# The last quarter of each row block ordered by products in the second layer of a dense network

## The chip, the cores and the metric

The kernel runs on one core of a Trainium2 chip. The metric is the device time of one execution in microseconds (us). Matmuls run on TensorE (PE, with its weight loads PEld), elementwise work on VectorE (DVE), ScalarE (ACT) and GpSimd (POOL), and most transfers are issued by SyncE (SP).

## What is computed

Three networks in a row: attention with a window of 128, a mixture of eight experts with two chosen for each token, and a dense network with a squared ReLU. Only the last is touched, and of it the last product:

```python
def _moe2_ref(x, w_in, w_out):       # x: 2304 x 512
    h = x @ w_in                     # w_in: 512 x 2048
    r = np.maximum(h, 0.0)
    g = r * r
    return (g @ w_out).astype(np.float32)   # w_out: 2048 x 512
```

## The kernel before

Each of the two layers of the dense network is computed with a scheme of seven products in place of eight block products: sums and differences of quarters of the operands go in, and sums and differences of the seven results give the quarters of the output. The products are called P1 to P7; their order in the code is P1, P2, P6, P7, P5, P4, P3. Each product of two float32 operands is three matmuls ("passes": high part by high part, high by low, low by high), with operands split into a high and a low part beforehand (helper `mul_out`, L1201; one matmul gives 128x256).

The second layer goes through nine **row blocks** of 256 rows. A row block is named by s (0 to 2) and u (0 to 2). Its seven results are summed in four PSUM banks, each bank holding 512 columns:

- `b13`: P1 in its first half (columns 0:256), P3 in its second
- `b26`: P2 and P6
- `b7`: P7 alone
- `b45`: P4 in the first half, P5 in the second

Row blocks where 3s+u is even ("even": five of nine, the last one among them) have three banks of tag "a" (psa in the profile) and one of tag "c" (psc, which is b45). The odd ones have four halves of tag "b" (psb).

The inner dimension of a row block is taken in four **quarters** (`kk` = 0 to 3, called batches), and each quarter in two **halves** (`k` = 0, 1). A half of a quarter is one turn through the seven products, 21 matmuls; a quarter is 42 matmuls, and a row block 168. The left operands of a quarter lie in one of three buffers `GC` (in the tiles wc and ex); the weights `WP` lie in tiles wa, ha, wb, hb and xa. Which of these a matmul reads shows in its name: psc<-ha,ex is a matmul into b45 of an even row block with weights in ha.

After each product of each half a function `step()` runs side work that is keyed to a slot number, 14 slots to a quarter. The side work of the second layer prepares later quarters (line L872 in the profile): `g_load` (DMA into xb), `g_adds` (sums gs, on POOL or DVE), and `g_split` (ACT writes the high part, DVE the low part, into the buffer GC of the quarter after next). `g_split` has its four parts at slots 2, 5, 8 and 11 of a quarter; parts 0 and 2 are on ACT, parts 1 and 3 on DVE.

The **evictions** of a row block stand in the last half of the last quarter. `p1` is a copy of P1 by ACT (L1242). Then DVE makes x = p1 + (P2, P6) (L1244, 128x512), u3 = x + P7 (L1246), y = u3 + (P4, P5) (L1248, 128x512; then SP writes y out, L1249), x += P5 (L1250) and x += P3 (L1252; then SP writes x out, L1253). In an even row block each of these stands behind the product that it needs last, so that it runs beside the later products; in an odd one all stand behind the last product.

Every engine executes its instructions in the order of the code. Waits between engines are put in by the framework where tiles are shared. The tiles x, y and gs are drawn from one ring of six buffers.

```python
batches = [(0, u, 2 * p + kk) for p in range(2) for u in range(2) for kk in range(2)]
batches += [(s, u, kk) for s in range(NSB) for u in range(3) for kk in range(4) if s or u > 1]
...
def mul_out(p, home, k, kk, o, start, stop):
    for m, (gp, wp) in enumerate(PASSES):
        nc.tensor.matmul(o, (part(home, p[0], gp)[:, kk * 128:(kk + 1) * 128]), (part(WP[k], p[1], wp)),
                         start=start and m == 0, stop=stop and m == 2, skip_group_check=True)
...
for n in range(len(batches)):
    for m in range(2):
        if n + 3 < len(batches):
            on(end + 14 * n + (9 + 3 * m if n < 5 else 1 + 4 * m), g_adds, n + 3, "dve" if n < 5 else "pool", m)
    for m in range(4):
        on(end + 14 * n + (2, 5, 8, 11)[m], g_split, n + 2, m)
```

Of the kernel before, what the change touches and what calls it, by code (L numbers as in the profile page):

```python
# [11 lines left out]
F32 = mybir.dt.float32  # L12
# [4 lines left out]
AF = mybir.ActivationFunctionType  # L17
OP = mybir.AluOpType
# [3 lines left out]
N, DM = B * S, H * D  # L22
# [9 lines left out]
SB = 768  # L32
HALF = 384
# [16 lines left out]
def attn_moe_ffn(ctx: ExitStack, tc: tile.TileContext, qt, kt, vt, wgn, noise, w1, w2, w_in, w_out,  # L50
                 consts, out):
    nc = tc.nc
    PSUM, DRAM = bass.MemoryType.PSUM, bass.MemoryType.DRAM
    const = ctx.enter_context(tc.tile_pool(name="const", bufs=1))
    rows = ctx.enter_context(tc.tile_pool(name="rows", bufs=1))
# [15 lines left out]
    def bank(tag):  # L71
        if tag == "b":
            return psum.tile([128, 2, 512], F32, name="psb", tag="b", bufs=2)
        return psum.tile([128, 512], F32, name="ps" + tag, tag=tag, bufs={"a": 3, "c": 1}[tag])
# [145 lines left out]
    P2, PT, PX, XI, G = {}, {}, {}, {}, {}  # L220
# [294 lines left out]
    for p in range(NT // 2):  # L515
# [6 lines left out]
        o = v + 2 if end else v + 3  # L522
# [30 lines left out]
    for v in range(-2, NV + 3):  # L553
# [4 lines left out]
        if 0 <= v < NV:  # L558
            i, g = divmod(v, 2)
# [242 lines left out]
    P1, P2, P6, P5, P7, P4, P3 = (0, 0), (1, 1), (3, 5), (5, 3), (6, 6), (2, 4), (4, 2)  # L802
# [5 lines left out]
    def spot(t, c0, n):  # L808

        return t[:, c0:c0 + 512 * n].rearrange("p (s i n) -> p s i n", s=2, i=n)  # L810

    WP, XC, tmp = [None] * 8, [None] * 7, []
# [26 lines left out]
    def part(home, i, s):  # L839
        for i0, ap in reversed(home):  # L840
            if i >= i0:
                return ap[:, s, i - i0, :]
# [228 lines left out]
    GC = [[(0, spot(*a, 7))] for a in ((late["wc"], 0), (late["wc"], 3584), (late["ex"], 0))]  # L1071
# [45 lines left out]
    for s in range(NSB - 1):  # L1117
        for i in range(6):
            t, m = 6 * (s + 1) + i, 56 * s + 5 * i + 3
# [22 lines left out]
    def step():  # L1142
        for f, a in side.pop(slot[0], []):
            f(*a)
        slot[0] += 1
# [53 lines left out]
# [4 lines that stand above are left out]
# [11 lines left out]
    two = lambda ap: ap.rearrange("p (k n) -> p k n", k=2)  # L1214
    twice = lambda ap: ap[:, None, :].to_broadcast([128, 2, 256])
    for n, (s, u, kk) in enumerate(batches):
        if kk == 0:
            if (3 * s + u) % 2:
                t = [bank("b") for _ in range(2)]
                banks = [x[:, m, :] for x in t for m in range(2)]  # L1220
            else:
                banks = [bank("a") for _ in range(3)] + [bank("c")]
            BANKS[s, u] = banks
        b13, b26, b7, b45 = BANKS[s, u]
        for k in range(2):
            st, en = kk + k == 0, kk == 3 and k == 1
            for m, (p, o, lead) in enumerate(((P1, b13[:, 0:256], True), (P2, b26[:, 0:256], True),
                                              (P6, b26[:, 256:512], False), (P7, b7[:, 0:256], True),
                                              (P5, b45[:, 256:512], True), (P4, b45[:, 0:256], False),
                                              (P3, b13[:, 256:512], False))):  # L1230
                mul_out(p, GC[n % 3], 2 * kk + k, k, o, st and lead, en)
                if not en:
                    step()
                    continue

                late_ = (3 * s + u) % 2
                if m == 0:
                    p1, u3 = tmp[2 + late_][:, 0:256], tmp[late_][:, 0:256]
                    x, y = [rows.tile([128, DM], F32, name="x", tag="r", bufs=6) for _ in range(2)]
                    i = s * SB + u * 128  # L1240
                if m == (6 if late_ else 0):
                    nc.scalar.activation(out=p1, in_=b13[:, 0:256], func=AF.Copy)  # L1242
                if m == (6 if late_ else 2):
                    nc.vector.tensor_tensor(out=two(x), in0=twice(p1), in1=two(b26), op=OP.add)  # L1244
                if m == (6 if late_ else 3):
                    nc.vector.tensor_tensor(out=u3, in0=x[:, 256:512], in1=b7[:, 0:256], op=OP.add)  # L1246
                if m == (6 if late_ else 5):
                    nc.vector.tensor_tensor(out=two(y), in0=twice(u3), in1=two(b45), op=OP.add)  # L1248
                    nc.sync.dma_start(out=out[i + HALF:i + HALF + 128, :], in_=y)  # L1249
                    nc.vector.tensor_tensor(out=x[:, 256:512], in0=x[:, 256:512], in1=b45[:, 256:512], op=OP.add)  # L1250
                if m == 6:
                    nc.vector.tensor_tensor(out=x[:, 256:512], in0=x[:, 256:512], in1=b13[:, 256:512], op=OP.add)  # L1252
                    nc.sync.dma_start(out=out[i:i + 128, :], in_=x)  # L1253
                step()


def _consts():
# [53 lines left out]
```

## Time and profile before

| | us |
|---|---|
| three runs | 972.5, 975.42, 977.13 (median 975.42) |
| the profiled execution | 974.33 |
| its span, first to last instruction | 972.6 |
| second layer of the dense network, first matmul | 785.82 |
| last quarter of the five even row blocks begins | 811.19, 841.43, 881.75, 922.07, 962.39 |

Start times are counted from the start of the span. A matmul row gives the start of the first matmul and the time to the end of the last; matmuls overlap, so the distance of starts, not the duration, is what one costs. "idle before <-releaser" in a timeline row is how long the engine had nothing to do ahead of it, and what ended this.

### The profile page before, as it was taken

How to read it: one execution, taken by the hardware profiler on the slowest of the kernel's cores; microseconds unless marked ns; L12 is line 12 of the kernel's file. 1: busy time of each engine (PE TensorE's matmuls, PEld its weight loads, DVE VectorE, ACT ScalarE, POOL GpSimd, SP SyncE). 2: the span in 40 equal slices, each digit the busy share in tenths (PEclk: the TensorE clock that was granted, in tenths of full speed). 3: DMA queues.
4: the chain of work that ended last, by engine and by line, in shares of the span. 5: the costliest groups of instructions: out<-in, count | busy, mean ns of one | idle time of the engine just before them, and what ended most of it. 6: DMA issues, size and time to landing. Idle time of an engine off the chain costs nothing. (4 is left out here: it accounts for less than half of the span.)

```text
span 972.6 us, 19636 instructions
## 1 busy us (share of the span) xinstructions
PE 956.8 (98%) x7438; PEld 878.9 (90%) x7438; DVE 668.2 (69%) x1452; ACT 463.2 (48%) x887; POOL 401.8 (41%) x433
## 2 busy tenths in 40 slices
PE   9999999999999999999999999999999999999997
PEld 6777789898998989899898898999999999999997
DVE  5777754657686776757774436778577899877773
ACT  7778733334343443433343346655555564434341
POOL 1565542124232333415334032624211624888880
PEclk9999999999999999999999999999999999999999
DMA  9767525456667576656655453966537874443331
GB/s 324 283 213 271 176 89 155 143 172 215 204 212 233 165 238 193 236 186 210 203 196 192 149 174 94 300 197 175 163 102 222 234 230 156 152 137 125 130 109 44
DMA packets 118199, 180.00 MB, mean 185 GB/s; under 512 B 11232, under 2 KB 66288, under 8 KB 117712
## 3 DMA queue, kind: packets, MB, share of 16 engines
q1 hardware_dynamic: 107120, 146.77, 46.8%
q0 software_dynamic: 10976, 31.90, 10.5%
q8 instruction: 59, 0.97, 0.4%
q14 instruction: 44, 0.36, 0.1%
HBM read 124.33 MB, written 54.30 MB: 184 GB/s over the span
## 5 line engine op out<-in xcount | busy, mean ns | idle before, releaser
L476 ACT ACTIVATE ha<-psa 128x384 fp32r<-128x384 f32 x64 | 31.3, 491 | 94.8 <-PE psa L472 93.2
L872 POOL TENSOR_TENSOR gs<-xb 128x256 f32<-128x256 f32 x62 | 60.2, 992 | 29.3 <-DVE wc L872 15.4
L268 ACT ACTIVATE p<-p,mx 128x192 f32<-128x192 f32 x144 | 57.5, 450 | 27.4 <-DVE mx L262 26.6
L689 POOL TENSOR_TENSOR et<-ex,et 128x512 f32<-128x512 f32 x16 | 20.9, 1304 | 111.5 <-DVE ex L685 111.5
L710 POOL DMA_INDIRECT yr<-yg,pos x36 | 37.3, 1037 | 68.6 <-DVE ha L477 45.1
L477 DVE SCALAR_TENSOR_TENSOR ha<-psa,ha 128x384 fp32r<-128x384 f32 x64 | 35.4, 553 | 42.6 <-ACT ha L476 37.5
L472 PE MATMUL psa<-xa,wa 128*128 128x384 f32 x288 | 55.0, 343 | 0.0
L428 POOL DMA_INDIRECT slots<-tok,pos x36 | 35.0, 972 | 45.7 <-DVE rs L314 30.0
L886 POOL DMA_DIRECT2D raw<-w x49 | 27.2, 561 | 63.5 <-DVE wb L872 18.4
L441 POOL DMA_INDIRECT xr<-xd,gidx x40 | 44.8, 1119 | 20.9 <-issue 6.1
L472 PE MATMUL psa<-xa,wc 128*128 128x384 f32 x288 | 53.3, 335 | 0.0
L791 PE MATMUL psb<-wa,ha 128*128 128x512 f32 x216 | 52.8, 396 | 0.0
L472 PEld LDWEIGHTS psa<-xa,wa 128*128 128x128 f32 x288 | 51.0, 194 | 0.2
L262 DVE CUSTOM_DVE_ANT_0 p<-psb,bias 128x192 f32<-128x192 f32 x144 | 45.8, 352 | 6.1 <-PE psb L257 5.4
L472 PEld LDWEIGHTS psa<-xa,wc 128*128 128x128 f32 x288 | 49.6, 188 | 0.2
L795 ACT ACTIVATE yo<-psb 128x512 f32<-128x512 f32 x38 | 22.7, 598 | 54.4 <-PE psb L791 38.7
L791 PEld LDWEIGHTS psb<-wa,ha 128*128 128x128 f32 x216 | 39.5, 188 | 7.8
L689 POOL TENSOR_TENSOR ex<-ex 128x512 f32<-128x512 f32 x12 | 15.6, 1302 | 74.6 <-DVE ex L685 74.6
L791 PE MATMUL psb<-wb,ha 128*128 128x512 f32 x176 | 46.3, 397 | 0.0
L110 DVE TENSOR_TENSOR wa<-raw,wa 128x1024 fp32r<-128x1024 f32 x20 | 25.7, 1284 | 29.4 <-ACT wa L106 29.3
L872 DVE TENSOR_TENSOR wc<-gs,wc 128x512 fp32r<-128x512 f32 x48 | 44.4, 965 | 0.4 <-ACT wc L872 0.4
L303 PEld LDWEIGHTS psb<-v,pt 64*64 64x64 f32 (+1 forms) x1056 | 32.8, 135 | 11.0 <-issue 7.7
(330 smaller groups left out, 2726.9 us busy)
## 6 DMA issues: line engine op xcount, KB each, us to landing
raw<-in_w_dram SPq DMA_DIRECT2D x64, 512.0 KB, 4.9
xb<-gmid SPq DMA_DIRECT2D x72, 256.0 KB, 2.9
v<-in_vt_dram SPq DMA_DIRECT2D x20, 520.0 KB, 5.3
yg<-yo SPq DMA_DIRECT2D x40, 256.0 KB, 3.1
raw<-w POOLq DMA_DIRECT2D x36, 256.0 KB, 3.8
gmid<-yo SPq DMA_DIRECT2D x48, 192.0 KB, 3.2
ex<-in_w_in_dram SPq DMA_DIRECT2D x16, 512.0 KB, 4.1
ex<-in_w_out_dram SPq DMA_DIRECT2D x16, 512.0 KB, 3.5
```

Of the source, the lines that this page charges most:

```text
L262: nc.vector.tensor_tensor_reduce(out=p2[j][:, a, :], in0=ps[:, a, j, :], in1=bias[:, 4 * g + 2 * j + a, :], op0=OP.add, op1=OP.min, scale= ...
L268: nc.scalar.activation(out=p2[j][:, a, :], in_=p2[j][:, a, :], func=AF.Exp, bias=mx[j][:, a:a + 1], scale=-1.0)
L303: nc.tensor.matmul(px[64 * x:64 * x + 64, a, j, :], l, r, start=not any(m[:2] == (x, a) for m in mms[:n]), stop=not any(m[:3] == (x, a, j) ...
L428: st = nc.gpsimd.indirect_dma_start(out=slots, out_offset=bass.IndirectOffsetOnAxis(ap=pos[:, i, k:k + 1], axis=0), in_=tok[:, i:i + 1], i ...
L441: nc.gpsimd.indirect_dma_start(out=XR[e, j], out_offset=None, in_=xd[0:PARTS[j] * 128] if early else xd, in_offset=bass.IndirectOffsetOnAx ...
L472: nc.tensor.matmul(o, w[wp][:, f * 128:(f + 1) * 128], x[:, xp, d, :], start=(n == 0), stop=(n == 11))
L476: nc.scalar.activation(out=hi, in_=ps, func=AF.Relu)
L477: nc.vector.scalar_tensor_tensor(out=lo, in0=ps, scalar=0.0, in1=hi.bitcast(F32), op0=OP.max, op1=OP.subtract)
L689: nc.gpsimd.tensor_tensor(out=x, in0=af, in1=cf, op=OP.add)
L710: nc.gpsimd.indirect_dma_start(out=YR[i, k], out_offset=None, in_=yg, in_offset=bass.IndirectOffsetOnAxis(ap=pos[:, i, k:k + 1], axis=0))
L791: nc.tensor.matmul(py, h[:, hq], wc[wp][:, wsl], start=(f + n == 0), stop=(f == 7 and n == 2))
L872: f(**a)
```

## The change

In the last quarter of each row block (kk = 3) the two halves of one product now stand in a row: P1 k=0, P1 k=1, P2 k=0, P2 k=1, and so on, instead of all products of k=0 and then all of k=1. The first three quarters are as before. The evictions still stand behind the k=1 half of the product that they need, which is now reached earlier for all but the last. The addition x += P5 gets a place of its own behind P5 (m = 4), ahead of y, where it stood behind y (m = 5) before. In the changed kernel it is L1248, y is L1250 (its DMA L1251), and the last addition L1253 (its DMA L1254).

```diff
-        for k in range(2):
+        prods = list(enumerate(((P1, b13[:, 0:256], True), (P2, b26[:, 0:256], True), (P6, b26[:, 256:512], False),
+                                (P7, b7[:, 0:256], True), (P5, b45[:, 256:512], True), (P4, b45[:, 0:256], False),
+                                (P3, b13[:, 256:512], False))))
+        turns = [(k, q) for q in prods for k in range(2)] if kk == 3 else [(k, q) for k in range(2) for q in prods]
+        for k, (m, (p, o, lead)) in turns:
             st, en = kk + k == 0, kk == 3 and k == 1
-            for m, (p, o, lead) in enumerate(((P1, b13[:, 0:256], True), (P2, b26[:, 0:256], True),
-                                              (P6, b26[:, 256:512], False), (P7, b7[:, 0:256], True),
-                                              (P5, b45[:, 256:512], True), (P4, b45[:, 0:256], False),
-                                              (P3, b13[:, 256:512], False))):
...
+            if m == (6 if late_ else 4):
+                nc.vector.tensor_tensor(out=x[:, 256:512], in0=x[:, 256:512], in1=b45[:, 256:512], op=OP.add)
+            if m == (6 if late_ else 5):
+                nc.vector.tensor_tensor(out=two(y), in0=twice(u3), in1=two(b45), op=OP.add)
+                nc.sync.dma_start(out=out[i + HALF:i + HALF + 128, :], in_=y)
...
-                if m == (6 if late_ else 5):
-                    nc.vector.tensor_tensor(out=two(y), in0=twice(u3), in1=two(b45), op=OP.add)
-                    nc.sync.dma_start(out=out[i + HALF:i + HALF + 128, :], in_=y)
-                    nc.vector.tensor_tensor(out=x[:, 256:512], in0=x[:, 256:512], in1=b45[:, 256:512], op=OP.add)
```

What stands in the queues, first on PE at the very end of the program, the last 24 matmuls and more of the last row block, with the waits that the instructions carry ("waits DVE_49" is a wait for a count that DVE raises). Before:

```order
L1201 MATMUL psc<-wa,ex 128x256 x6
L1201 MATMUL psa<-wa,ex 128x256 x3
L1201 MATMUL psa<-ha,ex 128x256 x6
L1201 MATMUL psa<-wa,ex 128x256 x6
L1201 MATMUL psc<-ha,ex 128x256 x6
L1201 MATMUL psa<-ha,ex 128x256 [waits Activation_49]
L1201 MATMUL psa<-ha,ex 128x256 x2
```

These are P5 and P4 of k=0 (x6), P3 of k=0, then the seven products of k=1; only the last of these, P3, carries a wait. The same place in the changed kernel, from the second half of P7 on:

```order
L1201 MATMUL psa<-wa,ex 128x256 x3
L1201 MATMUL psc<-wa,ex 128x256 x3
L1201 MATMUL psc<-ha,ex 128x256 x3
L1201 MATMUL psc<-wa,ex 128x256 [waits DVE_49]
L1201 MATMUL psc<-wa,ex 128x256 x2
L1201 MATMUL psc<-ha,ex 128x256 x3
L1201 MATMUL psa<-wa,ex 128x256 [waits Activation_49]
L1201 MATMUL psa<-wa,ex 128x256 x2
L1201 MATMUL psa<-ha,ex 128x256 x3
```

The rows are P7, P5 (two halves), P4 (two halves) and P3 (two halves); the first matmul of P4 now carries a wait for DVE, and that of P3 one for ACT a half earlier than before. The wait for DVE at this place is there in each of the five even row blocks and in no odd one.

On DVE the first even row block, as a piece of the difference (the row L872 with 128x2x3x128 is part 1 of `g_split`, L872 x2 its part 3):

```order
-L872 TENSOR_TENSOR wc<-xb,wc 128x2x3x128
 L1244 TENSOR_TENSOR x<-wt,psa 128x512
+L872 TENSOR_TENSOR wc<-xb,wc 128x2x3x128
 L1246 TENSOR_TENSOR tt<-x,psa 128x256
-L872 TENSOR_TENSOR wc<-gs,wc 128x512 x2
-L1248 TENSOR_TENSOR x<-tt,psc 128x512
-L1250 TENSOR_TENSOR x<-x,psc 128x256
-L1252 TENSOR_TENSOR x<-x,psa 128x256
+L1248 TENSOR_TENSOR x<-x,psc 128x256
+L1250 TENSOR_TENSOR x<-tt,psc 128x512
+L872 TENSOR_TENSOR wc<-gs,wc 128x512 x2
+L1253 TENSOR_TENSOR x<-x,psa 128x256
```

Part 1 of the split now stands behind the first eviction and part 3 behind y. The second, third and fourth even row blocks read the same; the last has no split left. In an odd row block only x += P5 and y change places. On ACT the copy L1242 moves ahead of part 0 of the split in the four even row blocks that have one. The order on SP and POOL is the same as before.

## Rows read from the trace of the kernel before

**Rows 1.** Page, part 1: busy time, share of span, instructions.
```profile
PE 956.8 (98%) x7438; PEld 878.9 (90%) x7438; DVE 668.2 (69%) x1452; ACT 463.2 (48%) x887; POOL 401.8 (41%) x433
```

**Rows 2.** Groups of PE instructions from 785 us on: busy, mean ns, idle before.
```profile
L1201 PE MATMUL psb<-wa,wc 128*128 128x256 f32 x144 | 18.4, 283 | 0.0
...
L1201 PE MATMUL psc<-xa,ex 128*128 128x256 f32 x6 | 0.9, 283 | 0.0
```

**Rows 3.** Timeline of the end, 960 to 973: start, us, instruction, idle before.
```profile
962.39 1.60 PE L1201 MATMUL psa<-wa,ex 128*128 128x256 f32 x12
...
965.47 0.38 ACT L1242 ACTIVATE wt<-psa 128x256 f32<-128x256 f32 x1 [11.55 <-PE psa L1201]
...
966.62 0.69 DVE L1244 TENSOR_TENSOR x<-wt,psa 128x512 f32<-128x512 f32 x1 [11.55 <-ACT wt L1242]
...
967.07 0.52 PE L1201 MATMUL psa<-ha,ex 128*128 128x256 f32 x3
967.41 0.42 DVE L1246 TENSOR_TENSOR tt<-x,psa 128x256 f32<-128x256 f32 x1
967.92 0.69 DVE L1248 TENSOR_TENSOR x<-tt,psc 128x512 f32<-128x512 f32 x1
968.53 0.41 DVE L1250 TENSOR_TENSOR x<-x,psc 128x256 f32<-128x256 f32 x1
...
969.05 0.42 DVE L1252 TENSOR_TENSOR x<-x,psa 128x256 f32<-128x256 f32 x1
969.50 0.33 SPq L1253 DMA_DIRECT2D out_dram<-x  x1
```

**Rows 4.** Timeline of PE, fourth even row block, where its last quarter begins.
```profile
922.07 1.60 PE L1201 MATMUL psa<-wa,wc 128*128 128x256 f32 x12
```

**Rows 5.** Timeline of DVE, fourth even row block.
```profile
925.93 0.69 DVE L1244 TENSOR_TENSOR x<-wt,psa 128x512 f32<-128x512 f32 x1 [2.02 <-PE psa L1201]
```

**Rows 6.** Timeline, 783 to 784: a matmul that waited for ACT.
```profile
783.09 0.49 ACT L1176 ACTIVATE tt<-psa 128x384 f32<-128x384 f32 x1 [0.18 <-PE psa L1046]
...
783.63 0.61 PE L1046 MATMUL psa<-ex,ha 128*128 128x384 f32 x2 [0.58 <-ACT tt L1176]
```

**Rows 7.** Timeline of PE, first even row block, where its last quarter begins.
```profile
811.19 1.60 PE L1201 MATMUL psa<-wa,ex 128*128 128x256 f32 x12
```

**Rows 8.** Timeline of DVE, first even row block.
```profile
815.77 0.42 DVE L872 TENSOR_TENSOR gs<-xb,gs 128x256 f32<-128x256 f32 x1
816.12 0.95 DVE L872 TENSOR_TENSOR wc<-xb,wc 128x768 fp32r<-128x768 f32 x1
816.98 0.68 DVE L1244 TENSOR_TENSOR x<-wt,psa 128x512 f32<-128x512 f32 x1
```

**Rows 9.** Timeline of POOL, first even row block.
```profile
818.87 1.82 POOL L872 TENSOR_TENSOR gs<-xb 128x256 f32<-128x256 f32 x2 [5.29 <-DVE wc L872]
```

**Rows 10.** Timeline of ACT, second even row block.
```profile
841.15 0.84 ACT L872 ACTIVATE wc<-xb 128x768 fp32r<-128x768 f32 x1 [2.74 <-PE psc L1201]
```

**Rows 11.** Timeline of DVE, second even row block.
```profile
842.03 1.24 DVE L872 TENSOR_TENSOR wc<-xb,wc 128x768 fp32r<-128x768 f32 x1 [1.69 <-ACT wc L872]
```

**Rows 12.** Timeline of POOL, second even row block.
```profile
841.71 2.15 POOL L872 TENSOR_TENSOR gs<-xb 128x256 f32<-128x256 f32 x2
```

**Rows 13.** Stretches: length, busy of PE, PEld, DVE, ACT, POOL; granted clock; DMA share, GB/s.
```profile
131.00:134.50 3.50, 2.08 (x19) 1.36 (x20) 1.24 (x3) 1.09 (x2) 2.90 (x6) 1.00 0.23 75
134.50:138.00 3.50, 3.50 (x13) 3.48 (x12) 1.19 (x10) 0.40 (x2) 1.04 (x2) 0.51 0.59 175
138.00:141.40 3.40, 3.40 (x29) 3.26 (x28) 2.22 (x13) 0.98 (x2) 0.64 (x1) 1.00 0.36 134
967.60:970.70 3.10, 0.00 (x0) 0.00 (x0) 1.67 (x4) 0.00 (x0) 0.00 (x0) 1.00 0.35 129
970.70:972.60 1.90, 0.00 (x0) 0.00 (x0) 0.00 (x0) 0.00 (x0) 0.00 (x0) 0.52 0.18 66
556.00:558.00 2.00, 1.18 (x6) 0.70 (x5) 0.51 (x2) 0.62 (x2) 0.00 (x0) 1.00 0.33 85
```

More of the change, by code (lines that the diff above doesn't have):

```diff
@@ L1224, in attn_moe_ffn @@
         b13, b26, b7, b45 = BANKS[s, u]
-        for k in range(2):
-            st, en = kk + k == 0, kk == 3 and k == 1
-            for m, (p, o, lead) in enumerate(((P1, b13[:, 0:256], True), (P2, b26[:, 0:256], True),
-                                              (P6, b26[:, 256:512], False), (P7, b7[:, 0:256], True),
-                                              (P5, b45[:, 256:512], True), (P4, b45[:, 0:256], False),
-                                              (P3, b13[:, 256:512], False))):
[L1231 to L1246, printed above, removed]
-                if m == (6 if late_ else 5):
-                    nc.vector.tensor_tensor(out=two(y), in0=twice(u3), in1=two(b45), op=OP.add)
-                    nc.sync.dma_start(out=out[i + HALF:i + HALF + 128, :], in_=y)
-                    nc.vector.tensor_tensor(out=x[:, 256:512], in0=x[:, 256:512], in1=b45[:, 256:512], op=OP.add)
-                if m == 6:
-                    nc.vector.tensor_tensor(out=x[:, 256:512], in0=x[:, 256:512], in1=b13[:, 256:512], op=OP.add)
-                    nc.sync.dma_start(out=out[i:i + 128, :], in_=x)
-                step()
@@ new lines, in attn_moe_ffn @@
+        prods = list(enumerate(((P1, b13[:, 0:256], True), (P2, b26[:, 0:256], True), (P6, b26[:, 256:512], False),
[3 more added lines that the diff above has]
+        for k, (m, (p, o, lead)) in turns:
+            st, en = kk + k == 0, kk == 3 and k == 1
+            mul_out(p, GC[n % 3], 2 * kk + k, k, o, st and lead, en)
+            if not en:
+                step()
+                continue
+            late_ = (3 * s + u) % 2
+            if m == 0:
+                p1, u3 = tmp[2 + late_][:, 0:256], tmp[late_][:, 0:256]
+                x, y = [rows.tile([128, DM], F32, name="x", tag="r", bufs=6) for _ in range(2)]
+                i = s * SB + u * 128
+            if m == (6 if late_ else 0):
+                nc.scalar.activation(out=p1, in_=b13[:, 0:256], func=AF.Copy)
+            if m == (6 if late_ else 2):
+                nc.vector.tensor_tensor(out=two(x), in0=twice(p1), in1=two(b26), op=OP.add)
+            if m == (6 if late_ else 3):
+                nc.vector.tensor_tensor(out=u3, in0=x[:, 256:512], in1=b7[:, 0:256], op=OP.add)
+            if m == (6 if late_ else 4):
[3 more added lines that the diff above has]
+                nc.sync.dma_start(out=out[i + HALF:i + HALF + 128, :], in_=y)
+            if m == 6:
+                nc.vector.tensor_tensor(out=x[:, 256:512], in0=x[:, 256:512], in1=b13[:, 256:512], op=OP.add)
+                nc.sync.dma_start(out=out[i:i + 128, :], in_=x)
+            step()
```

## The prediction

> **What bounds the kernel now.** I began with the page's busy shares: PE is busy 98% of the span and the next engine 69% [rows 1]. Then the groups of PE instructions of the second layer: no matmul of it had any idle time ahead [rows 2]. So up to its last matmul this stage lasts as long as its matmuls, and a wait of PE here goes into the time in full. Last I read the timeline of the end [rows 3]. The last quarter of the last row block begins at 962.39, and its last three matmuls at 967.07, which is 39 matmuls later: 0.12 each. The last ends at 967.07 + 0.52 = 967.59. DVE then still has four additions to do, because the first of them (L1244) began at 966.62 only, and the five follow each other; the last ends at 969.05 + 0.42 = 969.47, 1.88 after PE. The last transfer is issued at 969.50. The span of 972.6 ends about 3.1 after the last addition, and 1.7 lies around it in the execution of 974.33. That execution is 1.1 under the median of 975.42, so the median of other runs may lie that much above my sums.
>
> **What costs nothing.** The matmuls are the same ones with the same operands, and each has its own weight load before and after. The spacing is 0.12 across changes of bank and of product alike, so another order costs nothing as such. In odd row blocks every eviction stays behind the last product; only two DVE additions change places, y goes out one addition (0.41 [rows 3]) later, and SP has other row blocks' transfers only. On ACT the copy L1242 moves ahead of part 0 of the split. The copy can begin when both halves of P1 are done (five spacings and 0.28 after the quarter's start), takes 0.38, and the split 0.84 [rows 10], so the split is done about 2.1 into the quarter. DVE reaches its part at about 3.0 (below): 0.9 of cover; without it, DVE would start that much later. P3's earlier wait for ACT is for that copy, done 3 us before. No transfer changes its place on SP, and POOL's order is unchanged; but x and y now take buffers of the ring ahead of gs, so POOL's additions can begin later in such a quarter and run beside DVE.
>
> **What is gained.** Behind the last matmul only one addition has to remain instead of four. If PE ended as before, the last addition would begin 0.10 after 967.59 (0.10 is the delay of L1244 behind its product in the fourth even row block: the product ends at 922.07 + 29 × 0.12 + 0.28 = 925.83 [rows 4], the addition begins at 925.93 [rows 5]) and end at 968.11 instead of 969.47: 1.36 gained.
>
> **What is added.** The addition x += P5 (L1248 now) reads the second half of bank b45 as soon as P5 is done; the next matmuls, those of P4, write the first half of the same bank. The queue of PE shows a wait for DVE on the first of them in the five even row blocks. Before, DVE touched b45 only behind P4, and P4 carried no such wait. I take it that the wait is for this very addition, although the halves don't overlap. The sign for it in the kernel before: P3 of the last half, which writes the second half of b13, carries a wait for ACT, whose only use of b13 is the copy of its first half. So the waits go by bank. No row of before shows PE stopped by such a wait: there the copy ended at 965.47 + 0.38 and P3 came at 967.07 [rows 3]. The Trainium skill, PSUM — Partial Sum Buffer, section "PSUM bank collisions raise a hardware error", says that PSUM has to be guarded by bank and quarter of the partitions, not by address. By that rule the stall below belongs to the change wherever the addition stands between P5 and P4; by addresses there would be none and the sum would be 973.0. No run here shows yet which of them holds.
>
> Behind the waiting matmul on PE stand the rest of P4, P3 and every later row block; for P4 and P3 wait y and the last addition on DVE, and for the later matmuls ACT's splits, which only come later by as much. The stall is PE's start of P4 against 30 × 0.12 = 3.60 after the quarter's start.
>
> The least: P5's last matmul ends 0.28 after its start, where P4 would start 0.12 after it; DVE begins 0.10 later, takes 0.41, and PE follows 0.05 behind (783.58 to 783.63 [rows 6]). 0.16 + 0.10 + 0.41 + 0.05 = 0.72. More, where DVE gets to the addition later, since L1244, L1246 and part 1 of the split stand ahead of it:
>
> - Second to fourth even row block, with the fourth's times: P6 is done at 922.07 + 17 × 0.12 + 0.28 = 924.39, L1244 begins at 924.49, the split 0.61 later (as L1250 behind L1248 [rows 3]) at 925.10, L1246 0.86 behind that (the distance of 816.12 and 816.98 [rows 8]) at 925.96, L1248 0.51 later [rows 3] at 926.47; it ends at 926.88 and PE goes on at 926.93 instead of 925.67: 1.26. With POOL at work beside it (841.71 [rows 12]) the split took 1.24 instead of 0.95 [rows 8, 11], which would make it 1.55. I take 1.26, since the split now comes 3 us into the quarter and not at 0.6 as there, three times: 3.78 (2.16 to 4.65).
> - First even row block: here DVE is behind. Before, L1244 began at 816.98, though its product was done at 811.19 + 29 × 0.12 + 0.28 = 814.95 [rows 7, 8]. Its additions for other quarters still stand ahead, up to 815.77 + 0.42, so L1244 can begin at 816.12, where the split began. Then 816.73 for the split, 817.88 for L1246 (1.24, since POOL, which before idled 5.29 here [rows 9], comes later and may run beside it; 0.29 less without), 818.39 for L1248, 818.80 for its end, 818.85 for PE, instead of 814.79: 4.06 (3.77 to 4.1; 1.26 if DVE should not be behind).
> - Last row block: no split. P6 is done at 964.71, and L1244 began 0.47 behind P6 here (966.62 against 966.15), which I keep: 965.18. L1246 0.79 later, L1248 0.51 later at 966.48, its end 966.89, PE at 966.94 instead of 965.99. P3 ends at 966.94 + 11 × 0.12 + 0.28 = 968.54. y waits for P4 (967.82), and runs 967.92 to 968.61. The last addition runs from 968.64 to 969.06 instead of 969.47: 0.41 less. Of the gain of 1.36, 0.95 is gone.
>
> Sum: 4.06 + 3.78 − 0.41 = 7.43 slower.
>
> **The clock.** PE idle for 4 us touches its clock. Behind the last matmul PE did nothing; the clock stayed at 1.00 to 970.7 and was 0.52 after that. From 131.0 to 134.5 PE was idle for 1.42 of 3.50 us, and then the clock was 0.51 for 3.5 us of full work, and 1.00 again behind that. From 556 to 558 PE was idle for 0.82, and the clock stayed at 1.00 [rows 13]. The stall of 4.06 is longer than what came ahead of either fall, so I take one fall there, at the price of the second: 3.5 us at 0.51, 1.72 lost. The stalls of 1.26 lie between 0.82 (no fall) and 1.42 (fall); I take none. The levels are 1.2 and 2.4 GHz. The Trainium skill, TensorE: Matmul & The Clock Gate, section "Part 1: The HAM clock gate", says that idleness throttles the engine and sustained work releases it; the rows agree with that (0.52 behind idleness, 1.00 behind 3.5 us of work).
>
> So: 974.33 + 7.43 + 1.72 = 983.5.
>
> **The rivals.**
> - The stalls, but no fall of the clock: 974.33 + 7.43 = 981.8. For it: the clock stayed at 1.00 through 3.1 us of idleness at the end. Against it: 131 to 134.5.
> - The clock falls at all four long stalls: 983.5 + 3 × 1.72 = 988.6. For it the fall after 1.42, against it the 0.82 without one.
> - Every stall at its least, DVE in time everywhere: 4 × 0.72, and in the last row block 0.72 − 1.36; +2.2, 976.6. Against it: DVE's queue, and its delay in the first row block.
> - Not slower: P4's wait is for an older count of DVE that has long been reached. It decides at the value of that one wait: if it stands for anything ahead of L1248, no stall is left, and the gain at the end is all there is: 974.33 − 1.36 = 973.0. Against it: the wait appears just where L1248 was put, and nowhere else.
>
> **How the numbers follow.** About 0.5% (4.9 us) is what a measurement here can tell from no change. Chances: forecast 0.48, no fall 0.27, falls everywhere 0.08, least stalls 0.10, no wait 0.07. The range leaves out the last two (0.17): from 979.0 (the first row block with 1.26 like the others, and no fall: 974.33 + 4 × 1.26 − 0.41) to 988.6. Slower by over 0.5%: the first three, 0.83, less 0.03 because 981.8 is only 2.5 over the bound and runs of before spread over 4.6; within: 0.18; faster 0.02, since even 973.0 is only 0.25% down and only spread would make more of it.
>
> **What would show it.** In the profile after, PE matmuls of psc at P4 should have idle time ahead, released by DVE x L1248: some 4 us at 815, 1.3 three times, 0.9 at the end; in odd row blocks none. The granted clock should show about 0.5 for some 3 us behind the first. The last addition should end about 0.5 after the last matmul. I am wrong if PE shows no idle time at P4, if DVE is not behind in the first even row block, or if the clock stays at 1.00.

## The result and the profile after

| | before | after |
|---|---|---|
| median of six runs each | 973.48 | 981.15 (979.74 to 982.78) |
| profiled execution (span) | 974.33 (972.6) | 979.74 (978.0) |
| second layer: first matmul to end of span | 785.82 to 972.6: 186.78 | 785.19 to 978.0: 192.81 |

The ratio is 1.0064, 95% interval 1.0045 to 1.0083: slower, clear of no change. (The two medians alone would give 1.0079, inside this interval.) A second measurement of the same kernel (below) gave 1.0081, 1.0066 to 1.0096. The forecast was 983.5 with a range of 979.0 to 988.6.

First the waits of PE in the changed kernel: who waited for what, us in total, how often, the longest.

```profile
PE psc L1201 <- DVE x L1248: 6.0, 5, 2.1
PE psc L387 <- DVE oh L375: 3.3, 5, 1.5
```

The first row is new. It is the longest wait of PE in the program, in a stage that had none [rows 2]. The groups of the second layer in the changed kernel put it on two groups, those of bank b45 (psc) with weights in wa; the other groups still show 0.0:

```profile
L1201 PE MATMUL psb<-wa,wc 128*128 128x256 f32 x144 | 19.9, 283 | 0.0
...
L1201 PE MATMUL psc<-wa,wc 128*128 128x256 f32 x36 | 5.8, 289 | 2.3 <-DVE x L1248 2.3
...
L1201 PE MATMUL psc<-wa,ex 128*128 128x256 f32 x24 | 4.3, 295 | 3.8 <-DVE x L1248 3.8
```

Then the timeline of the changed kernel in the first, the fourth and the last even row block, PE and DVE around the wait:

```profile
813.05 0.84 DVE L872 TENSOR_TENSOR gs<-xb,gs 128x256 f32<-128x256 f32 x1
813.61 0.52 PE L1201 MATMUL psc<-ha,ex 128*128 128x256 f32 x3
813.82 0.68 DVE L1244 TENSOR_TENSOR x<-wt,psa 128x512 f32<-128x512 f32 x1
814.41 0.94 DVE L872 TENSOR_TENSOR wc<-xb,wc 128x768 fp32r<-128x768 f32 x1
815.28 0.41 DVE L1246 TENSOR_TENSOR tt<-x,psa 128x256 f32<-128x256 f32 x1
815.80 0.42 DVE L1248 TENSOR_TENSOR x<-x,psc 128x256 f32<-128x256 f32 x1
816.27 0.62 PE L1201 MATMUL psc<-wa,ex 128*128 128x256 f32 x3 [2.14 <-DVE x L1248]
816.73 0.52 PE L1201 MATMUL psc<-ha,ex 128*128 128x256 f32 x3
...
928.83 0.69 DVE L1244 TENSOR_TENSOR x<-wt,psa 128x512 f32<-128x512 f32 x1 [3.51 <-ACT ex L872]
929.43 0.95 DVE L872 TENSOR_TENSOR ex<-xb,ex 128x768 fp32r<-128x768 f32 x1
929.65 0.52 PE L1201 MATMUL psc<-ha,wc 128*128 128x256 f32 x3
930.30 0.41 DVE L1246 TENSOR_TENSOR tt<-x,psa 128x256 f32<-128x256 f32 x1
930.82 0.42 DVE L1248 TENSOR_TENSOR x<-x,psc 128x256 f32<-128x256 f32 x1
931.30 0.62 PE L1201 MATMUL psc<-wa,wc 128*128 128x256 f32 x3 [1.12 <-DVE x L1248]
...
970.53 0.69 DVE L1244 TENSOR_TENSOR x<-wt,psa 128x512 f32<-128x512 f32 x1 [9.74 <-issue]
971.35 0.52 PE L1201 MATMUL psc<-ha,ex 128*128 128x256 f32 x3
971.91 0.42 DVE L1248 TENSOR_TENSOR x<-x,psc 128x256 f32<-128x256 f32 x1 [0.17 <-PE psc L1201]
972.39 0.62 PE L1201 MATMUL psc<-wa,ex 128*128 128x256 f32 x3 [0.51 <-DVE x L1248]
973.57 0.52 PE L1201 MATMUL psa<-ha,ex 128*128 128x256 f32 x3
974.12 0.42 DVE L1253 TENSOR_TENSOR x<-x,psa 128x256 f32<-128x256 f32 x1
```

In each place the row of PE just ahead of the wait is the second half of P5. P4 would start three spacings (0.36) behind that row's start. So the stalls are 816.27 − 813.97 = 2.30 in the first row block, 931.30 − 930.01 = 1.29 in the fourth, and 972.39 − 971.71 = 0.68 in the last; the second and third (847.89 and 889.59) give 1.29 and 1.28. That is 6.84. (The idle time in brackets is 0.16 less, because it counts from the end of the last matmul.) After each stall the first three matmuls take 0.46 to the next row instead of 0.36: 0.1 five times, called the refill below. The rows of the weight loads (PEld) suggest where it comes from; here those of the fourth row block for the first half of P5 and for P4:

```profile
929.18 0.43 PEld L1201 LDWEIGHTS psc<-wa,wc 128*128 128x128 f32 x3
...
931.30 0.41 PEld L1201 LDWEIGHTS psc<-wa,wc 128*128 128x128 f32 x3 [1.33 <-DVE x L1248]
```

In the stream the load of these weights begins 0.11 ahead of its matmul (929.18 against 929.29). Behind the wait both begin at 931.30, so the load was held back as well and nothing ran ahead. No run tried this apart.

At the end the last matmul is over at 974.09 and the last addition at 974.54: 0.45 behind, where it was 1.88 [rows 3]. From the end of that addition to the end of the span it is 3.46, before 3.13. So the second layer's matmuls span 188.90 instead of 181.77, and what follows them 3.91 instead of 5.01; together 6.03 longer. (Stalls and refills make 7.34, not the 7.13 of the matmuls, because the last quarter of the first row block begins 25.18 behind the first matmul here and began 25.37 behind it before; a second profile of the kernel before, below, has 25.18 too.) The rest of the program, which the change doesn't touch, was 0.63 shorter in this execution. The fall of the clock at 134.5 [rows 13], 1.72 by the forecast's price, was absent here; what took back the other part wasn't followed up.

### The profile page after: what moved, and what is told of

Read it like the earlier page. It is cut to its first block, busy times and chain, and to the rows that moved or that the text cites. A ratio compares the mean times of both kernels' runs of the same rounds, so it can differ in the third digit from the quotient of the medians.

```text
span 978.0 us, 19624 instructions
## 1 busy us (share of the span) xinstructions
PE 956.6 (98%) x7438; PEld 877.9 (90%) x7438; DVE 665.7 (68%) x1452; ACT 463.5 (47%) x887; POOL 400.0 (41%) x433
## 5 line engine op out<-in xcount | busy, mean ns | idle before, releaser
L872 POOL TENSOR_TENSOR gs<-xb 128x256 f32<-128x256 f32 x62 | 60.2, 991 | 35.6 <-DVE wc L872 21.0
L872 DVE TENSOR_TENSOR wc<-gs,wc 128x512 fp32r<-128x512 f32 x48 | 44.9, 976 | 0.0
```

Source lines behind the costliest of these rows:

```text
L872: f(**a)
```

## The experiments

Theory A is that of the prediction: the loss is P4's wait, since x += P5 reads the other half of its bank, and the length of the wait is DVE's queue; the order by products costs nothing by itself and shortens the end. Its rivals are B, that the order itself costs PE time, and those named with each run. The first four runs were on a chip where the kernel before took 998.8 us, the others on one where it took 973.4; in the profiles the difference lies ahead of the experts (their first matmul with tile xa is at 158.4 in the first of these runs and at 134.4 in the kernel before). So ratios are to the kernel before on the same chip, and I also compare the second layer from its first matmul to the end of the span, which the early stages don't touch.

**The order alone** (`e1_add_at_5`), with x += P5 behind P4:

```diff
-            if m == (6 if late_ else 4):
+            if m == (6 if late_ else 5):
```

> The changed kernel, except that x += P5 stands with y behind P4 (m = 5, ahead of y), so that nothing reads the bank b45 between P5 and P4. Theory A (the stall is P4's wait for the addition that reads the other half of its bank; the order by products is free): no idle time of PE at P4 in any row block, and the end shorter than in the kernel before: y and the additions follow P4, the last addition ends some 0.75 us behind the last matmul instead of 1.88, so about 1.1 us (0.1%) faster than the kernel before, and some 7 us faster than the changed one. Theory B (the order by products itself costs PE time, by its changes of weights tile or by six matmuls into one place): still 4 to 7 us slower than the kernel before.

Measured: ratio 1.0015 (0.9992 to 1.0039); second layer 808.32 to 994.2, 185.88. I ran it once more on the other chip.

> The order by products with x += P5 behind P4, once more. Theory A: no stall, second layer about 0.9 us shorter than in the kernel before, which is 0.1% of the time and can lie inside the interval; the interval should hold 0.999 and not 1.005. Theory B (the order itself costs): 1.004 or more.

Measured: ratio 0.9997 (0.9982 to 1.0011); second layer 787.42 to 973.3, 185.88 again, against 186.78 in the first and 186.54 in the second profile of the kernel before. One of its groups of PE, the matmuls that had waited for 3.8 in the changed kernel, and its end:

```profile
L1201 PE MATMUL psc<-wa,ex 128*128 128x256 f32 x24 | 4.0, 283 | 0.0
```
```profile
968.33 0.42 DVE L1248 TENSOR_TENSOR x<-x,psc 128x256 f32<-128x256 f32 x1 [0.89 <-PE psc L1201]
968.49 0.52 PE L1201 MATMUL psa<-ha,ex 128*128 128x256 f32 x3
968.66 0.68 DVE L1250 TENSOR_TENSOR x<-tt,psc 128x512 f32<-128x512 f32 x1
969.26 0.41 DVE L1253 TENSOR_TENSOR x<-x,psa 128x256 f32<-128x256 f32 x1
```

x += P5 now waits for PE, and PE for nobody. The last addition is over 0.66 behind the last matmul. B is out: the new order with its changes of weights is as fast as the old one, and the 0.7 to 0.9 us that the stage gains is too little for the ratio to show.

**The addition alone** (`e2_add_early_old_order`), the products in the old order:

```diff
-        turns = [(k, q) for q in prods for k in range(2)] if kk == 3 else [(k, q) for k in range(2) for q in prods]
+        turns = [(k, q) for k in range(2) for q in prods]
```

> The order of products of the kernel before (all of one half first), with x += P5 in its place behind P5 (m = 4). Theory A: the stall is there without the new order, at P4 of the second half, in the five even row blocks: DVE's chain L1244, L1246, L1248 ends about 5.6 us into the quarter, P4 is due at 4.32, so 1.3 us in the three middle ones, 2 to 3 in the first, 1.7 in the last; the end gains nothing that covers it, so 6 to 9 us slower than the kernel before. Theory B: the order is the old one, so within 1 us of the kernel before.

Measured: ratio 1.0069 (1.004 to 1.0099); second layer 194.31, 7.5 more than before. PE's rows with idle time:

```profile
838.11 0.62 PE L1201 MATMUL psc<-ha,ex 128*128 128x256 f32 x3 [2.26 <-DVE x L1248]
...
869.78 0.62 PE L1201 MATMUL psc<-ha,ex 128*128 128x256 f32 x3 [1.17 <-DVE x L1248]
...
995.38 0.62 PE L1201 MATMUL psc<-ha,ex 128*128 128x256 f32 x3 [1.54 <-DVE x L1248]
```

The stalls are 2.42, three of 1.33 and 1.70 (0.16 added), as expected. The last of them holds some luck. L1244 came 0.09 behind P6 there, not 0.47 as in the first profile of the kernel before, but DVE then stood still for 0.47 between L1246 and the addition, which it did in none of the other four even row blocks:

```profile
994.91 0.42 DVE L1248 TENSOR_TENSOR x<-x,psc 128x256 f32<-128x256 f32 x1 [0.47 <-DVE tt L1246]
```

The end did gain something, other than expected: the last addition ends 0.70 behind the last matmul instead of 1.88, so the stalls and refills (8.6) went into the stage with 7.5 only. One addition, moved past one product, is the whole loss.

**The split behind the addition** (`e3_split_behind`), to shorten DVE's queue:

```diff
-            on(end + 14 * n + (2, 5, 8, 11)[m], g_split, n + 2, m)
+            on(end + 14 * n + ((2, 9, 10, 11) if batches[n][2] == 3 else (2, 5, 8, 11))[m], g_split, n + 2, m)
```

> The changed kernel with part 1 of the split moved from slot 5 to slot 9 of the last quarters (parts 2 and 3 to 10 and 11), so that on DVE it stands behind x += P5. Theory A: the stall is as long as DVE's queue ahead of the addition. Without the split ahead the middle row blocks should stall 0.7 to 0.8 us instead of 1.29, as the last one does (0.68), and the first one 0.9 less; about 2.4 us faster than the changed kernel, 3 to 4 us slower than the kernel before. Theory A2 (the stall is a fixed cost of such a wait, whatever is queued): the middle ones stay at 1.29.

Measured: ratio 1.0063 (1.0028 to 1.0098), too wide to place it; second layer 807.09 to 997.5, 190.41, so 3.6 more than before and 2.4 less than the first profile of the changed kernel.

```profile
837.61 0.62 PE L1201 MATMUL psc<-wa,ex 128*128 128x256 f32 x3 [1.57 <-DVE x L1248]
...
868.62 0.62 PE L1201 MATMUL psc<-wa,ex 128*128 128x256 f32 x3 [0.52 <-DVE x L1248]
```

The second to fifth stall are all 0.51 or 0.52 of idle time now, 0.68 with the 0.16. The first is 1.73, which is 0.57 less than in the first profile of the changed kernel; 0.9 was expected. So the stall is what DVE has queued ahead of the addition, down to a floor: wait for P5, addition, go on.

**P4 in another bank** (`e4_p4_other_bank`): the free second half of b7 holds P4, and y is made by two additions.

```diff
-                                (P7, b7[:, 0:256], True), (P5, b45[:, 256:512], True), (P4, b45[:, 0:256], False),
+                                (P7, b7[:, 0:256], True), (P5, b45[:, 256:512], True), (P4, b7[:, 256:512], False),
...
+                nc.vector.tensor_tensor(out=y[:, 256:512], in0=u3, in1=b45[:, 256:512], op=OP.add)
...
-                nc.vector.tensor_tensor(out=two(y), in0=twice(u3), in1=two(b45), op=OP.add)
+                nc.vector.tensor_tensor(out=y[:, 0:256], in0=u3, in1=b7[:, 256:512], op=OP.add)
```

> The changed kernel with P4 summed in the free second half of b7 instead of the first half of b45, and y made by two additions of 256 columns. Theory A with waits by bank: P4 no longer waits for x += P5 (b45), but for u3 (L1246), the addition that reads the first half of its new bank, which ends about 0.5 us earlier: stalls of about 0.75 in the middle row blocks, with L1246 named as what ended them. If waits went by address, or P4 waited for L1248 for another reason than its bank, there would be either no stall at all or the same 1.29 behind L1248. About 2.5 us faster than the changed kernel by the first reading.

Measured: ratio 1.0071 (1.0042 to 1.01); second layer 812.64 to 1004.9, 192.26. PE's rows with idle time, and PE at the lower clock (stretches as in [rows 13]):

```profile
843.85 0.62 PE L1201 MATMUL psa<-wa,ex 128*128 128x256 f32 x3 [2.27 <-DVE tt L1246]
...
876.43 0.62 PE L1201 MATMUL psa<-wa,ex 128*128 128x256 f32 x3 [0.60 <-DVE tt L1246]
```
```profile
841.60:843.80 2.20, 0.00 (x0) 0.00 (x0) 2.19 (x4) 1.15 (x2) 0.12 (x1) 1.00 0.00 0
844.80:848.00 3.20, 3.20 (x17) 3.20 (x17) 3.00 (x6) 1.99 (x3) 1.89 (x2) 0.51 0.70 256
848.20:852.00 3.80, 3.80 (x34) 3.80 (x33) 2.13 (x2) 0.32 (x1) 3.72 (x5) 1.00 0.56 170
```

The wait went with the bank: P4 now waits for L1246, which reads P7 in the first half of b7, and no longer for L1248; the middle stalls are 0.76 instead of 1.29. The halves don't overlap here either, so the kernel's waits go by bank and not by address. (In the even row blocks each bank is a tile of its own, so bank and tile are not told apart by any run.) The time gained was not what I expected, because the clock fell to 0.51 behind the first stall in this execution, and because that stall was 2.43, no shorter than in the changed kernel.

**The changed kernel once more** (`after_again`):

> The changed kernel once more, for what differs from execution to execution. Theory A: five stalls at P4 behind L1248 again, 1.3 us in the three middle row blocks and 0.5 to 0.7 in the last whatever the execution; the first one from 2 to 4 us, as far as DVE is behind there. If the granted clock falls behind the first stall, it costs about 1.5 us more in that execution. 5 to 9 us slower than the kernel before. If the first stall's size and the clock stay as in the first profile (2.1 us, clock 1.00), the spread of its times comes from elsewhere, as from the early stage.

Measured: ratio 1.0081 (1.0066 to 1.0096); second layer 786.81 to 981.4, 194.59, which is 1.78 more than in its first profile. The first row block in PE's timeline, and the clock:

```profile
815.24 0.52 PE L1201 MATMUL psc<-ha,ex 128*128 128x256 f32 x3
818.26 1.01 PE L1201 MATMUL psc<-wa,ex 128*128 128x256 f32 x3 [2.50 <-DVE x L1248]
819.06 0.84 PE L1201 MATMUL psc<-ha,ex 128*128 128x256 f32 x3
...
820.98 2.91 PE L1201 MATMUL psb<-ha,wc 128*128 128x256 f32 x21
```
```profile
815.70:818.30 2.60, 0.10 (x2) 0.04 (x1) 2.40 (x5) 1.15 (x2) 0.00 (x0) 0.96 0.00 0
818.30:820.70 2.40, 2.40 (x11) 2.40 (x12) 0.76 (x2) 0.84 (x1) 0.00 (x0) 0.50 0.67 219
821.70:825.00 3.30, 3.30 (x30) 3.30 (x29) 3.30 (x5) 0.54 (x2) 3.29 (x3) 1.00 0.54 187
```

The first stall is 2.66 (818.26 − 815.60) instead of 2.30, and behind it the clock is at 0.50. The 12 matmuls from 818.26 on take 2.72 instead of 1.44 and the next 21 take 2.75 instead of 2.52: 1.51, of which 0.1 is the refill. So 0.36 of longer stall and 1.41 of clock are the whole difference of 1.78. The four other stalls have the same idle times within 0.01.

**The last row block alone** (`e5_last_only`): both parts of the change there, the old order elsewhere.

```diff
-        turns = [...] if kk == 3 else [...]
+        turns = [...] if kk == 3 and n == len(batches) - 1 else [...]
...
-            if m == (6 if late_ else 4):
+            if m == (6 if late_ else 4 if n == len(batches) - 1 else 5):
```

> The order by products and the early x += P5 in the last row block alone; all other row blocks in the order of the kernel before (there x += P5 stands with y, ahead of it). Theory A: one stall of 0.5 to 0.7 us in the last row block, the last addition ends about 0.45 behind the last matmul instead of 1.88, so some 0.7 us shorter than the kernel before: within 0.2% of it. Theory B': the loss of the change lies at its end, in the last row block: several us slower.

Measured: ratio 1.0004 (0.9989 to 1.0018); second layer 784.00 to 970.4, 186.40, so 0.38 shorter than in the first profile of the kernel before and 0.14 shorter than in the second; 0.7 was expected.

```profile
963.62 0.52 PE L1201 MATMUL psc<-ha,ex 128*128 128x256 f32 x3
964.48 0.42 DVE L1248 TENSOR_TENSOR x<-x,psc 128x256 f32<-128x256 f32 x1 [0.47 <-PE psc L1201]
964.96 0.62 PE L1201 MATMUL psc<-wa,ex 128*128 128x256 f32 x3 [0.82 <-DVE x L1248]
```

The loss is not at the end. The stall was 0.98 rather than 0.5 to 0.7, because DVE took up the addition 0.34 behind the end of P5, where 0.04 was enough in the changed kernel (971.87 to 971.91). DVE's idle time ahead of it is the same 0.47 as in the last row block of e2. What holds DVE up there I don't know.

**The kernel before once more** (`before_again`):

> The kernel before once more, for its profile on the same chip: no idle time of PE in the second layer, 186 to 187 us from its first matmul to the end of the span, and DVE behind by some 1 to 3 us at the first even row block's evictions.

Measured: 974.31; second layer 785.96 to 972.5, 186.54, no idle time of PE. In its first row block:

```profile
814.65 0.43 DVE L872 TENSOR_TENSOR gs<-xb,gs 128x256 f32<-128x256 f32 x1
815.00 0.95 DVE L872 TENSOR_TENSOR wc<-xb,wc 128x768 fp32r<-128x768 f32 x1
815.87 0.68 DVE L1244 TENSOR_TENSOR x<-wt,psa 128x512 f32<-128x512 f32 x1
```

The quarter begins at 811.14 here, so DVE was free for the evictions 3.86 into it; in the profile on which the forecast rested it was 4.93 [rows 7, 8].

## Why the prediction was right, and where its sizes were off

- **The wait of P4 by bank.** Right. Five stalls behind L1248, none in odd row blocks; three runs moved it by moving its cause (none without the early addition, five with that addition alone in the old order, and with P4 in another bank five behind L1246). By bank here means not by address; bank and tile are one in these row blocks. The Trainium skill, PSUM — Partial Sum Buffer, section "PSUM bank collisions raise a hardware error", asks for such guards by bank and partitions and not by address; the waits of this kernel agree with that (0.76 behind L1246 for a half that P4 doesn't touch). That the chip needs them was not tried.
- **Second to fourth row block**: forecast 3.78, measured 3.86. The sum over DVE's queue (distances of starts from other rows) held within 0.03 each, and POOL was not beside the split.
- **First row block**: forecast 4.06, measured 2.30, and this is the term that was mis-sized. L1244 began 3.45 into the quarter (813.82 − 810.37), not 4.93: 1.48. The split took 0.94, not 1.24: the other 0.28. I took DVE's delay of one profile for a property of the kernel. It comes from the stage's start. After that DVE has no idle time up to the first row block, so what it is late there it still is here. The first `wc<-gs` began 788.55 − 785.82 = 2.73 behind the first matmul in the kernel before and 786.47 − 785.19 = 1.28 in the changed one, which is 1.45 of the 1.48. In the second profile of the changed kernel it is 788.33 − 786.81 = 1.52, which is 0.24 of the 0.36 by which its first stall is longer. The second profile of the kernel before has 787.46 − 785.96 = 1.50. What set the profile of the forecast apart is a wait of DVE for a transfer just ahead, 0.95, which none of the other three profiles of the two kernels shows. Both profiles show this start; here the one of before and then that of after:

```profile
786.97 0.56 DVE L1065 TENSOR_TENSOR yo<-psb,wt 128x384 f32<-128x384 f32 x1 [0.95 <-DMA gmid<-yo]
...
788.55 1.29 DVE L872 TENSOR_TENSOR wc<-gs,wc 128x512 fp32r<-128x512 f32 x2 [0.44 <-ACT wc L872]
```
```profile
786.47 1.29 DVE L872 TENSOR_TENSOR wc<-gs,wc 128x512 fp32r<-128x512 f32 x2
```

- **The last row block**: forecast a stall of 0.95 and a last addition 0.52 behind the last matmul, measured 0.68 and 0.45. L1244 came 0.10 behind P6 as in the other row blocks, not 0.47 as in the profile before.
- **Two terms were missing from the sum**: the refill of 0.1 behind each stall, 0.5 in all, and the way from the last addition to the end of the span, 0.33 longer than before (3.46 against 3.13).
- **The clock**: forecast one fall for 1.72. In the first profile there was none, and a clock that stays at 1.00 is one of the prediction's own signs of being wrong; the rival without a fall held in that execution. In the second there was one for 1.41. Of the twelve executions of the changed kernel four show a mean granted clock of 1.000 (979.88 to 981.07 us), which leaves no room for such a fall. Of five profiles with a first stall of 1.73 us or more (two of the changed kernel, and e2, e3, e4) the fall is in two, behind 2.66 and 2.43; it is missing behind 2.30, 2.42 and 1.73. So it belongs to some executions and not to others; 2.42 without and 2.43 with a fall, in two different kernels, show that the length of the stall alone does not decide it, and what else does stays open. Of the two cases that I held apart, 981.8 and 983.5, both occur. That the forecast came close is in part luck: the likeliest case was 983.5, and in the terms measured here the sum would be 974.33 + 6.0 = 980.3 without a fall and 974.33 + 7.8 = 982.1 with one and the longer first stall. The median of 981.15 lies between; the first stall, forecast 1.76 too long, made the sum too high in either case.
- **What was costed at nothing**: right. The order by products (e1), ACT's copy ahead of the split, and the odd row blocks show no cost. POOL's later start in the quarter was seen, but beside the split it did nothing.

## What to carry to other kernels

Before an eviction is moved ahead to run beside later matmuls, look which bank the next matmuls write: here a read of one half held back the write of the other, and the engine that stood still was the busiest one. One product later the same addition cost nothing (e1). Such a stall is as long as the reader's queue, not as long as the read, so count everything queued ahead of it on that engine. And a delay that is read from one profile, where an engine works without a gap from some start on, carries the chance of that start with it; look at a second profile before it becomes the largest term of a sum.

## What was not expected of the hardware

The clock fell behind a single stall of 2.4 to 2.7 us in a stage that was otherwise full of matmuls (0.50 from 818.3 to 820.7, and 0.51 from 844.8 to 848.0), in some executions and not in others with a stall of nearly the same size (2.30 and 2.42). Behind a wait the first three matmuls took 0.10 longer than three in the stream do (0.46 against 0.36), and their first weight load began with the first matmul and not 0.11 ahead of it.
